# Order, engine and layout changes in a channel attention with two feed-forward networks: two tiles abreast at the start, differences on VectorE, w_in kept in the place of w1, and the last product turned round

## The chip, the cores and the metric

The kernel runs on one core of a Trainium2 chip. The time is device time in microseconds (us) of one execution; a kernel's time is the median of several runs. TensorE (PE) multiplies matrices and loads its weights in separate instructions (PEld), VectorE is DVE, ScalarE is ACT, GpSimd is POOL. SyncE (SP) issues all DMA transfers here. SBUF is the working memory, PSUM holds TensorE's results in eight banks of 128 x 512 float32.

## The reference

There are 6016 tokens of 256 channels. A channel attention gives a 256 x 256 matrix `a`, which multiplies `v`; the first network has 2048 inner columns, the second 1536:

```python
qn = q / (np.linalg.norm(q, axis=1, keepdims=True) + 1e-06)   # k likewise
s = kn.transpose(0, 2, 1) @ qn / tau
a = np.exp(s - s.max(-1, keepdims=True)); a /= a.sum(-1, keepdims=True) + 1e-09
x = v @ a                                    # 6016 x 256
h = x @ w_in                                 # 256 x 2048
g = np.where(h >= 1, h, np.where(h <= -1, 0, (h + 1) ** 2 / 4))
x = g @ w_out                                # 2048 x 256
xn = x / np.sqrt(np.mean(x * x, -1, keepdims=True) + 1e-06) * rms_g
out = (silu(xn @ w_gate) * (xn @ w_val)) @ w_out2   # 256 x 1536, 1536 x 256
```

The five weight matrices arrive as float64.

## The kernel before

**Products in three parts.** Each operand of the networks is kept as a high part in a format of 32 bits that TensorE takes in one pass (fp32r) and a low part, the difference. A product is three matmuls: high by high, high by low, low by high. `split` makes the two parts: a ScalarE copy gives the high one, a subtraction (`sub_hi`, line 86, on VectorE or GpSimd) the low one.

**Attention first.** 14 chunks of q and k are loaded; ScalarE squares them, VectorE sums the squares, TensorE accumulates the scores (line 298). The softmax follows on VectorE and ScalarE. As `v @ a @ w_in` is `v @ (a @ w_in)`, `make_w1` computes w1 = a w_in in four groups of 512 columns, each of two PSUM tiles with six matmuls (line 419).

**Weights.** `fetch` loads 512 KB of float64 (128 x 1024 words) into one of three wide buffers. `narrow` makes float32 of it with four VectorE instructions (lines 158, 162, 166, 174) and two of ScalarE (170, 180), and GpSimd subtracts the high part (line 182). That is one job; there are 34: 8 for w_in, 8 for w_out, 6 each for w_gate, w_val and w_out2. `pump` moves up to two jobs in flight by one stage each and starts one; a job takes five pumps. `require` pumps until given jobs are done. The results for w_in go to two of the eight buffers of a pool (`op`) that also holds the operands of the tiles, so no more than a few groups can wait.

**Tiles and blocks.** Tokens run in 12 tiles, eleven of 512 and one of 384. A tile has 16 blocks ("1", t, f) of the first network and 12 blocks ("2", t, f) of the second. A first block is `emit_A` (six matmuls, line 439), then Relu, Square and a VectorE instruction (lines 449 to 451, `start_g`), then a split (`finish_g`), and three blocks later `emit_B` (six matmuls, line 471). A second block is `emit_GV` (twelve matmuls, line 541), Silu and a product (552, 553), a split, and two blocks later `emit_D`. In `emit_D` the token block is the stationary operand: four blocks of 128 tokens, three matmuls each, 256 columns wide (line 573). `norm` (lines 479 to 524) makes the second network's input from a tile's sums; `prep_v` transposes and splits the next tile's v.

**Order.** A list, `order`, gives the blocks. The 16 first blocks of tile 0 and the first twelve of tile 1 run by themselves; six second blocks of tile 0 (`late`) go among the last four of tile 1. From then on tile t takes the last six second blocks of tile t-2 (`early`) into its first half and the first six of tile t-1 into its second. 18 second blocks are left at the end. After each block, `work` does one stage of a norm or a prep_v and `pump` one stage of the weights. The framework then orders each engine's queue by its own planned times, with the program's order as priority, so instructions can pass others that wait.

**PSUM.** Four banks hold results of A, GV and w1; one pair of banks (`ps_y`) the sums of B, one pair (`ps_o`) those of D.

Of the kernel before, what the change touches and what calls it, by code (L numbers as in the profile page):

```python
# [8 lines left out]
F32 = mybir.dt.float32  # L9
# [7 lines left out]
TOK = 512  # L17
SKEW = 6
LAG = 12
MID = 8  # L20
BLAG = 3
W1_AT = (0, 4, 8)
STAGE = 3
PRE = 2
FLIGHT = 2
# [3 lines left out]

QK_CHUNKS = (2, 2, 4, 4, 4, 4, 4, 4, 4, 4, 4, 3, 2, 2)  # L30

WIDE_MAX = 122879.9921875
# [3 lines left out]
def tile_channel_attention_two_ffn(  # L36
# [35 lines left out]
    ps_mm = ctx.enter_context(tc.tile_pool(name="ps_mm", bufs=4, space=bass.MemoryType.PSUM))  # L72
    ps_y = ctx.enter_context(tc.tile_pool(name="ps_y", bufs=1, space=bass.MemoryType.PSUM))
    ps_o = ctx.enter_context(tc.tile_pool(name="ps_o", bufs=1, space=bass.MemoryType.PSUM))

    def mm_tile(name):
        return ps_mm.tile([P, TOK], F32, tag="mm", name=name)

    def tmp_tile(name):
# [108 lines left out]
    later = []  # L188

# [4 lines left out]
    def narrow_job():  # L194
        if not wide:
            fetch()
        key, x, dst = wide.pop(0)
        if w1_done[0] >= 0:
            while jobs and len(wide) < STAGE - FLIGHT:
# [6 lines left out]
    w1_done = [-1]  # L206

    def may_start():
        key = wide[0][0] if wide else jobs[0][0] if jobs else None
        return key is not None and not (key[0] == "wi" and key[1] > w1_done[0] + 2)  # L210

    def pump():
        for job in flight[:]:
            if next(job, "end") == "end":
                flight.remove(job)
        if len(flight) < FLIGHT and may_start():
            job = narrow_job()
# [8 lines left out]

    wi = {}

    def wi_dst(g, c):
        def dst():  # L230
            if c == 0:
                wi[g] = [opp.tile([P, NC, TOK], F32R, tag="op", name=f"wi{g}_{i}") for i in range(2)]
            return wi[g][0][:, c, :], wi[g][1][:, c, :]
        return dst

# [9 lines left out]

    def wi_jobs(todo, g):
        for c in range(NC):
            todo.append((("wi", g, c), (w_in, c * P, 1), g * TOK, wi_dst(g, c)))

# [6 lines left out]
    NG = F1 // TOK  # L256
    for g in range(2):
        wi_jobs(jobs, g)
    wo_jobs(0)
    for g in range(2, NG):  # L260
        wi_jobs(later, g)
        wo_jobs(g - 1)
    wo_jobs(NG - 1)
    w2 = {}
    for g in range(F2 // TOK):
# [19 lines left out]
    acc = sp.tile([P, 2, JM, C], F32, name="acc")  # L285
    s_ps = [
        ps_y.tile([P, 2, TOK], F32, tag="y", name="s_ps0")[:, 0, :C],
        ps_o.tile([P, 2, 2, C], F32, tag="o", name="s_ps1")[:, 0, 0, :],
    ]
    NQ = len(QK_CHUNKS)  # L290
# [15 lines left out]
    for ci, nj in enumerate(QK_CHUNKS):  # L306
# [28 lines left out]
        if ci >= BEHIND:  # L335
            scores(ci - BEHIND, 1)
    for _ in range(PRE):
        fetch()
    load_v(0)
# [70 lines left out]

    def make_w1(g, b):
        h, l = wi[g]
        ah, al = at[b]
        ps = mm_tile(f"w1_ps{g}_{b}")
        i = 0
        for c in range(NC):
            sl = slice(c * P, (c + 1) * P)
            for x, w in ((ah, h), (ah, l), (al, h)):
                nc.tensor.matmul(ps, x[:, sl], w[:, c, :], start=(i == 0), stop=(i == 3 * NC - 1))
                i += 1  # L420
        sl = slice(g * TOK, (g + 1) * TOK)
        split(w1h[:, b, sl], w1l[:, b, sl], ps)
        if b == NC - 1:
            w1_done[0] = g
            del wi[g]

# [29 lines left out]
    def finish_g(t, f):  # L456
# [3 lines left out]
        gl = spl.tile([P, TOK], F32R, tag="gl", bufs=3, name=f"gl{t}_{f}")  # L460
        split(gh[:, :n], gl[:, :n], r[:, :n], nc.gpsimd if t < 2 or f < 3 else nc.vector)
        g_op[t, f] = (gh, gl)

    def emit_B(t, f):
        _, n = tiles[t]
        if f == 0:
            y_ps[t] = ps_y.tile([P, 2, TOK], F32, tag="y", name=f"y{t}")
        gh, gl = g_op.pop((t, f))
# [95 lines left out]
    def emit_D(t, f):  # L564
        _, n = tiles[t]
        if f == 0:
            o_ps[t] = ps_o.tile([P, 2, 2, C], F32, tag="o", name=f"o{t}")
        uh, ul = u_op.pop((t, f))
        wdh, wdl = w2["dh"], w2["dl"]
        for b in range(n // P):  # L570
            sl = slice(b * P, (b + 1) * P)
            for i, (x, w) in enumerate(((uh, wdh), (uh, wdl), (ul, wdh))):
                nc.tensor.matmul(  # L573
                    o_ps[t][:, b // 2, b % 2, :], x[:, sl], w[:, f, :],
                    start=(f == 0 and i == 0 and b % 2 == 0),
                    stop=(f == NF2 - 1 and i == 2),
                    skip_group_check=True,
                )

    def store(t):  # L580
        n0, n = tiles[t]
        o = o_ps.pop(t)
        nblk = n // P
        for h in range(2):
# [11 lines left out]

    order = []
    m2 = []
    for t in range(NT):
        if t:  # L600
            early, m2 = m2, [("2", t - 1, f) for f in range(NF2)]
            late, m2 = m2[:NF2 - SKEW], m2[NF2 - SKEW:]
        else:
            early, late = [], []
        mid = MID if early else LAG
        for f in range(NF1):
            order.append(("1", t, f))
            if f < mid:
                keep = len(early) * (mid - 1 - f) // mid
                if early:  # L610
                    keep = min(keep, SKEW * (mid - 1 - f) // mid)
                while len(early) > keep:
                    order.append(early.pop(0))
            else:
                keep = (NF2 - SKEW) * (NF1 - 1 - f) // (NF1 - mid)
                while len(late) > keep:
                    order.append(late.pop(0))
    order.append(("flush1",))
    order += m2
    order += [("2", NT - 1, f) for f in range(NF2)]  # L620

    tasks = []

    def work(n_stages=1):
        for _ in range(n_stages):
# [3 lines left out]
            if next(task, "end") == "end":  # L629
                tasks.remove(task)  # L630

    require(*[("wi", 0, c) for c in range(NC)])
    jobs.extend(later)
    for _ in v0:
        pass
    for b in range(NC):
        make_w1(0, b)
    m1, m2 = [], []

    def step1(t, f):  # L640
        if t == 0 and f in W1_AT:
            g = W1_AT.index(f) + 1
            require(*[("wi", g, c) for c in range(NC)])
            for b in range(NC):
                make_w1(g, b)
        ps = emit_A(t, f)
        m1.append((t, f))
        if len(m1) >= 2:
            finish_g(*m1[-2])
        start_g(t, f, ps)  # L650
        if len(m1) > BLAG:
            did_B(*m1[-1 - BLAG])

    def did_B(t, f):
        if t == 0:
            require(("wo", f // 2))
        emit_B(t, f)
        if f == NF1 - 1:
            tasks.insert(0, norm(t))

# [17 lines left out]

    for it in order:
        if it[0] == "1":  # L680
            _, t, f = it
            if f == 0 and t + 1 < NT:
                load_v(t + 1)
            if f == 8 and t + 1 < NT:
                tasks.append(prep_v(t + 1))
            step1(t, f)
            work(1)
            pump()
        elif it[0] == "2":
            while it[1] not in x_op:  # L690
                work(1)
            step2(*it[1:])
            work(1)
            pump()
        else:
            finish_g(*m1[-1])
            for i in range(BLAG, 0, -1):
                did_B(*m1[-i])
            work(2)
    finish_u(*m2[-1])  # L700
# [37 lines left out]
```

## Time and profile before

| | us |
|---|---|
| runs of the kernel | 1218.34, 1219.10, 1219.85 (median 1219.1) |
| the profiled execution: its time | 1220.48 |
| its span, first to last instruction | 1218.7 |
| PE, DVE, ACT, POOL busy in the span | 1179.0, 678.5, 638.3, 179.8 |

Matmuls are pipelined: one of 512 columns is listed with some 390 ns, but the next begins earlier. What one costs is read from the distance between starts, or from the chain of waits, which counts each stretch once. VectorE's entries overlap a little in the same way. A chain piece such as "1.36 PE y L471 x6" says that six matmuls took 1.36 us of the chain.

### The profile page before, as it was taken

What the parts mean: (1) busy time and instruction counts of PE and PEld (TensorE: products, weight loads), DVE (VectorE), ACT (ScalarE), POOL (GpSimd) and SP (SyncE); (2) the same over time, 40 slices, a digit from 0 to 9 for tenths busy, and PEclk for the clock granted to TensorE, in tenths of its full rate; (3) what the DMA queues carried; (4) which work ended last, traced back from release to release, by engine and by line L of the source; (5) the groups of instructions that cost most, each with busy time, mean ns of one, the idle gap of its engine ahead of it and who ended that gap; (6) DMA issues with size and microseconds to landing.
All of it is one profiled execution on the core that took longest, in us unless ns stands there. A gap on an engine that the chain in (4) does not pass through costs nothing.

```text
span 1218.7 us, 15601 instructions
## 1 busy us (share of the span) xinstructions
PE 1179.0 (97%) x6000; PEld 1010.6 (83%) x6000; DVE 678.5 (56%) x977; ACT 638.3 (52%) x1076; POOL 179.8 (15%) x128
## 2 busy tenths in 40 slices
PE   7888789999999999999999999999999999999998
PEld 6666567888888888888888888888888888899998
DVE  5899999464464464364365355355355345445443
ACT  6566776454464455454455455455445445445432
POOL 0255775110010010010010010010010010010000
PEclk9999899999999999999999999999999999999999
DMA  9734433010001001001001001001001000000000
GB/s 352 191 103 121 116 94 85 1 18 18 1 7 29 1 1 35 1 1 35 1 1 36 1 1 35 1 1 35 1 1 31 1 1 18 1 1 18 1 18 14
DMA packets 67275, 43.48 MB, mean 36 GB/s; under 512 B 51456, under 2 KB 57472, under 8 KB 67200
## 3 DMA queue, kind: packets, MB, share of 16 engines
q1 hardware_dynamic: 67200, 42.48, 12.4%
q8 instruction: 47, 0.77, 0.3%
q14 instruction: 28, 0.23, 0.1%
HBM read 36.31 MB, written 6.16 MB: 35 GB/s over the span
## 4 chain that ended last, share of the span: by engine, by line
PE 84%; DVE 7%; DMA 4%; issue 2%; ACT 1%; SPq 1%; POOL 0%; DVEq 0%; POOLq 0%; ACTq 0%
PE y L471 18%; PE h L439 18%; PE o L573 16%; PE vp L541 15%; PE gp L541 15%; DMA qk<-in_q_dram 2%; DVE wide L162 1%; DVE wide L174 1%; DVE wide L158 1%; DVE wide L166 1%; DVE g L451 1%; DMA wide<-in_moe_w_in_dram 1%; SPq L124 1%; DMA wide<-in_moe_w_out_dram 0%; DMA wide<-in_moe_w_val_dram 0%
## 5 line engine op out<-in xcount | busy, mean ns | idle before, releaser
L89 ACT ACTIVATE uh<-u 128x512 fp32r<-128x512 f32 (+1 forms) x144 | 89.8, 624 | 256.1 <-PE o L573 252.4
L86 POOL TENSOR_TENSOR gl<-g,gh 128x512 fp32r<-128x512 f32 (+1 forms) x62 | 85.6, 1384 | 833.0 <-ACT gh L89 619.8
L451 DVE SCALAR_TENSOR_TENSOR g<-h,g 128x512 f32<-128x512 f32 (+1 forms) x192 | 129.6, 676 | 121.6 <-ACT g L450 121.6
L86 DVE TENSOR_TENSOR ul<-u,uh 128x512 fp32r<-128x512 f32 (+1 forms) x144 | 99.2, 689 | 158.5 <-ACT uh L89 158.0
L553 DVE TENSOR_TENSOR u<-u,vp 128x512 f32<-128x512 f32 (+1 forms) x144 | 97.3, 676 | 136.2 <-PE vp L541 133.7
L89 ACT ACTIVATE gh<-g 128x512 fp32r<-128x512 f32 (+1 forms) x192 | 119.0, 620 | 91.6 <-DVE g L451 90.0
L449 ACT ACTIVATE g<-h 128x512 f32<-128x512 f32 (+1 forms) x192 | 112.5, 586 | 93.7 <-PE h L439 92.5
L573 PE MATMUL o<-wdh,ul 128*128 128x256 f32 x564 | 159.6, 283 | 0.0
L573 PE MATMUL o<-wdl,uh 128*128 128x256 f32 x564 | 159.5, 283 | 0.0
L573 PE MATMUL o<-wdh,uh 128*128 128x256 f32 x564 | 158.8, 282 | 0.0
L439 PE MATMUL h<-vh,w1h 128*128 128x512 f32 (+1 forms) x384 | 150.1, 391 | 8.1 <-DVE g L451 7.8
L471 PE MATMUL y<-gh,woh 128*128 128x512 f32 (+1 forms) x384 | 149.7, 390 | 5.4 <-DVE x L485 4.7
L471 PE MATMUL y<-gl,woh 128*128 128x512 f32 (+1 forms) x384 | 149.8, 390 | 1.9 <-POOL gl L86 1.9
L439 PE MATMUL h<-vh,w1l 128*128 128x512 f32 (+1 forms) x384 | 149.3, 389 | 0.0
L471 PE MATMUL y<-gh,wol 128*128 128x512 f32 (+1 forms) x384 | 149.2, 389 | 0.0
L439 PE MATMUL h<-vl,w1h 128*128 128x512 f32 (+1 forms) x384 | 148.3, 386 | 0.0
L86 DVE TENSOR_TENSOR gl<-g,gh 128x512 fp32r<-128x512 f32 (+1 forms) x130 | 91.1, 701 | 76.5 <-ACT gh L89 75.2
L450 ACT ACTIVATE g<-g 128x512 f32<-128x512 f32 (+1 forms) x192 | 119.0, 620 | 4.4
L541 PE MATMUL gp<-xh,wgh 128*128 128x512 f32 (+1 forms) x288 | 111.7, 388 | 3.8 <-DVE g L451 3.6
L541 PE MATMUL vp<-xh,wvh 128*128 128x512 f32 (+1 forms) x288 | 111.2, 386 | 1.6 <-ACT u L552 1.6
L573 PEld LDWEIGHTS o<-wdl,uh 128*128 128x128 f32 x564 | 107.6, 191 | 5.1
L573 PEld LDWEIGHTS o<-wdh,uh 128*128 128x128 f32 x564 | 107.5, 191 | 5.0
(109 smaller groups left out, 2053.3 us busy)
## 6 DMA issues: line engine op xcount, KB each, us to landing
wide<-in_moe_w_out_dram SPq DMA_DIRECT2D x14, 512.0 KB, 3.7
out_dram<-ob SPq DMA_DIRECT2D x23, 256.0 KB, 2.2
vin<-in_v_dram SPq DMA_DIRECT2D x88, 64.0 KB, 2.5
qk<-in_q_dram SPq DMA_DIRECT2D x9, 512.0 KB, 10.2
qk<-in_k_dram SPq DMA_DIRECT2D x9, 512.0 KB, 10.2
wide<-in_moe_w_in_dram SPq DMA_DIRECT2D x8, 512.0 KB, 4.6
wide<-in_moe_w_gate_dram SPq DMA_DIRECT2D x6, 512.0 KB, 3.6
wide<-in_moe_w_val_dram SPq DMA_DIRECT2D x6, 512.0 KB, 3.6
```

What stands on the lines that cost most here:

```text
L86: (eng or nc.vector).tensor_tensor(out=dst_lo, in0=src, in1=hi.bitcast(F32), op=ALU.subtract)
L89: nc.scalar.activation(out=dst_hi, in_=src, func=AF.Copy)
L124: nc.sync.dma_start(out=xv[32 * a:32 * a + 32, c, :n // 32, :], in_=src[a, c])
L158: nc.vector.tensor_scalar(out=high.bitcast(F32), in0=high.bitcast(F32), scalar1=WIDE_MAX, scalar2=-WIDE_MAX, op0=ALU.min, op1=ALU.max,)
L439: nc.tensor.matmul(ps[:, :n], w[:, c, f * P:(f + 1) * P], x[:, c, :n], start=(i == 0), stop=(i == 3 * NC - 1),)
L449: nc.scalar.activation(out=r[:, :n], in_=ps[:, :n], func=AF.Relu, bias=0.5, scale=0.5)
L450: nc.scalar.activation(out=r[:, :n], in_=r[:, :n], func=AF.Square)
L451: nc.vector.scalar_tensor_tensor(out=r[:, :n], in0=ps[:, :n], scalar=1.0, in1=r[:, :n], op0=ALU.max, op1=ALU.min)
L471: nc.tensor.matmul(y_ps[t][:, c, :n], w[:, f, c * P:(c + 1) * P], x[:, :n], start=(f == 0 and i == 0), stop=(f == NF1 - 1 and i == 2),)
L541: nc.tensor.matmul(ps[:, :n], w[:, c, f * P:(f + 1) * P], x[:, c, :n], start=(i == 0), stop=(i == 3 * NC - 1),)
L553: nc.vector.tensor_tensor(out=u[:, :n], in0=u[:, :n], in1=ps[1][:, :n], op=ALU.mult)
L573: nc.tensor.matmul(o_ps[t][:, b // 2, b % 2, :], x[:, sl], w[:, f, :], start=(f == 0 and i == 0 and b % 2 == 0), stop=(f == NF2 - 1 and i ...
```

## The change

The scores' two banks, y and o now come from one pool of two pairs. The jobs for w_in write groups 1 to 3 into `w1h` and `w1l` themselves, where `make_w1` later writes w1; so all eight can be done early, and `PUMPS` lets ten pumps run while q and k are still loaded. The low part of a narrowed weight is taken on VectorE, and that of g on VectorE except for f < 3 of tiles past 3. The blocks of tiles 0 and 1 alternate; the second network begins after four blocks of tile 2 and stays two tiles behind; after the first network's last block 24 second blocks are left. Each block now has one pump, each third block two. D has the weights as the stationary operand (six matmuls 512 wide) except in the last tile, so its result has channels on partitions; `store` transposes it in blocks of 32 x 32 on VectorE and writes it with eight transfers in pieces of 128 bytes, as v is read.

```diff
+PAIR = (1.5, 19.0)
+ALONE = 4
+HELD = 4
-PRE = 2
+PUMPS = (0, 0, 0, 0, 0, 0, 0, 2, 2, 2, 2, 2, 0, 0)
-    ps_y = ctx.enter_context(tc.tile_pool(name="ps_y", bufs=1, space=bass.MemoryType.PSUM))
-    ps_o = ctx.enter_context(tc.tile_pool(name="ps_o", bufs=1, space=bass.MemoryType.PSUM))
+    ps_yo = ctx.enter_context(tc.tile_pool(name="ps_yo", bufs=2, space=bass.MemoryType.PSUM))
...
-        nc.gpsimd.tensor_tensor(out=lo, in0=got, in1=hi.bitcast(F32), op=ALU.subtract)
+        sub_hi(lo, got, hi)
...
+    wi = {0: [opp.tile([P, NC, TOK], F32R, tag="op", name=f"wi{i}") for i in range(2)]}
+    for g in range(1, F1 // TOK):
+        wi[g] = [w[:, :, g * TOK:(g + 1) * TOK] for w in (w1h, w1l)]
...
+    for g in range(NG):
+        wi_jobs(g)
+        wo_jobs(g)
...
         if ci >= BEHIND:
             scores(ci - BEHIND, 1)
-    for _ in range(PRE):
-        fetch()
+        for _ in range(PUMPS[ci]):
+            pump()
...
-        split(gh[:, :n], gl[:, :n], r[:, :n], nc.gpsimd if t < 2 or f < 3 else nc.vector)
+        split(gh[:, :n], gl[:, :n], r[:, :n], nc.gpsimd if t > 3 and f < 3 else nc.vector)
...
+        for c in range(NC):
+            sl = slice(c * P, (c + 1) * P)
+            for i, (w, x) in enumerate(((wdh, uh), (wdl, uh), (wdh, ul))):
                 nc.tensor.matmul(
-                    o_ps[t][:, b // 2, b % 2, :], x[:, sl], w[:, f, :],
+                    o_ps[t][:, c, :n], w[:, f, sl], x[:, :n],
+                    start=(f == 0 and i == 0), stop=(f == NF2 - 1 and i == 2),
                 )
...
+        if t < NT - 1:
+            dst = out[n0:n0 + n, :].rearrange("(b j) (c a i) -> a c j b i", j=32, c=NC, a=4, i=32)
+            for c in range(NC):
+                ob = tmp_tile(f"ob{t}_{c}")
+                nc.vector.transpose(out=ob[:, :n], in_=o[:, c, :n])
+                src = ob.rearrange("p (b i) -> p b i", i=32)
+                for a in range(4):
+                    nc.sync.dma_start(out=dst[a, c], in_=src[32 * a:32 * a + 32, :n // 32, :])
+            return
...
+    at_block = [((f, 0), ("1", 0, f)) for f in range(NF1)]
+    for f in range(NF1):
+        at_block.append(((PAIR[0] + f * (PAIR[1] - PAIR[0]) / (NF1 - 1), 1), ("1", 1, f)))
+    order = [block for _, block in sorted(at_block)]
+    second = [("2", t, f) for t in range(NT) for f in range(NF2)]
+    done = 0
+    for t in range(2, NT):
+        first = ALONE if t == 2 else 0
+        n = NF2 - HELD if t == 2 else NF2 + HELD if t == 3 else NF2
+        base = done
         for f in range(NF1):
             order.append(("1", t, f))
+            while done < base + n * (f + 1 - first) // (NF1 - first):
+                order.append(second[done])
+                done += 1
+    order += [("B",)] * BLAG
+    order += second[done:]
...
+        work(1)
+        pump()
+        if i % 3 == 0:
             pump()
```

## Rows read from the trace of the kernel before

**Rows 1.** The page's 40 slices: VectorE's busy tenths, TensorE's granted clock.
```profile
DVE  5899999464464464364365355355355345445443
PEclk9999899999999999999999999999999999999999
```

**Rows 2.** TensorE's waits from 57.8 to 215 us, first and last of nine.
```profile
PE h L439 <- DVE g L451: 7.8, 7, 1.8
...
PE gp L541 <- ACT u L552: 0.3, 1, 0.3
```

**Rows 3.** The chain that ended last: start us, us, what.
```profile
351.37 2.04 PE h L439 x9
...
547.91 1.43 PE o L573 x12
549.34 1.39 PE h L439 x6
550.73 1.36 PE y L471 x6
...
1010.68 2.04 PE h L439 x9
```

**Rows 4.** TensorE's first w1 matmul and last o matmul, in order of time.
```profile
57.79 2.07 PE L419 MATMUL w_ps<-wi,ah 128*128 128x512 f32 x4
...
1214.40 0.28 PE L573 MATMUL o<-wdh,ul 128*128 128x256 f32 x1
```

**Rows 5.** VectorE's narrowing by line, 57.7 to 205 us: count | busy us, mean ns.
```profile
L166 DVE SCALAR_TENSOR_TENSOR wide<-wide 128x512 uint32<-128x512 uint32 x30 | 30.8, 1028 | 0.2
L174 DVE SCALAR_TENSOR_TENSOR wide<-wide 128x512 uint32<-128x512 uint32 x29 | 28.7, 991 | 0.8 <-ACT wide L170 0.6
L162 DVE TENSOR_SCALAR wide<-wide 128x512 uint32<-128x512 uint32 x30 | 23.6, 786 | 0.0
L158 DVE TENSOR_SCALAR wide<-wide 128x512 f32<-128x512 f32 x30 | 23.2, 774 | 2.8 <-DMA wide<-in_moe_w_in_dram 1.6 <-DMA wide<-in_moe_w_out_dram 0.6 <-DMA wide<-in_moe_w_val_dram 0.5
```

**Rows 6.** VectorE in order of time, 60.68 to 62.57 us, GpSimd idle.
```profile
60.68 0.70 DVE L174 SCALAR_TENSOR_TENSOR wide<-wide 128x512 uint32<-128x512 uint32 x1
61.30 0.68 DVE L166 SCALAR_TENSOR_TENSOR wide<-wide 128x512 uint32<-128x512 uint32 x1
61.90 0.42 DVE L158 TENSOR_SCALAR wide<-wide 128x512 f32<-128x512 f32 x1
62.23 0.42 DVE L162 TENSOR_SCALAR wide<-wide 128x512 uint32<-128x512 uint32 x1
62.57 0.68 DVE L86 TENSOR_TENSOR w1l<-w_ps,w1h 128x512 fp32r<-128x512 f32 x1
```

**Rows 7.** VectorE and GpSimd in order of time around 74 us.
```profile
74.00 1.53 POOL L86 TENSOR_TENSOR gl<-g,gh 128x512 fp32r<-128x512 f32 x1 [0.24 <-ACT gh L89]
74.30 1.78 DVE L174 SCALAR_TENSOR_TENSOR wide<-wide 128x512 uint32<-128x512 uint32 x1
```

**Rows 8.** DMA issues on SyncE's queue, in order of time.
```profile
22.81 0.33 SPq L147 DMA_DIRECT2D wide<-in_moe_w_in_dram  x1
24.14 0.33 SPq L310 DMA_DIRECT2D qk<-in_q_dram  x1
...
28.15 8.82 SPq L124 DMA_DIRECT2D vin<-in_v_dram  x5
37.08 0.42 SPq L310 DMA_DIRECT2D qk<-in_q_dram  x1
```

**Rows 9.** The instructions on the tile vin: duration ns min/median/max.
```profile
L124 SPq DMA_DIRECT2D vin<-in_v_dram x96: 315/487/3522, 28.2 to 931.5; - x96
```

**Rows 10.** One ScalarE line, 57.7 to 205 us.
```profile
L450 ACT ACTIVATE g<-g 128x512 f32<-128x512 f32 x31 | 19.2, 624 | 0.3
```

**Rows 11.** The page's DMA issues: count, KB each, median us to landing.
```profile
out_dram<-ob SPq DMA_DIRECT2D x23, 256.0 KB, 2.2
vin<-in_v_dram SPq DMA_DIRECT2D x88, 64.0 KB, 2.5
```

More of the change, by code (lines that the diff above doesn't have):

```diff
@@ L17 @@
 TOK = 512
-SKEW = 6
-LAG = 12
-MID = 8
+PAIR = (1.5, 19.0)
+ALONE = 4
+HELD = 4
 BLAG = 3
@@ L72, in tile_channel_attention_two_ffn, with yo_tile @@
     ps_mm = ctx.enter_context(tc.tile_pool(name="ps_mm", bufs=4, space=bass.MemoryType.PSUM))
-    ps_y = ctx.enter_context(tc.tile_pool(name="ps_y", bufs=1, space=bass.MemoryType.PSUM))
-    ps_o = ctx.enter_context(tc.tile_pool(name="ps_o", bufs=1, space=bass.MemoryType.PSUM))
+    ps_yo = ctx.enter_context(tc.tile_pool(name="ps_yo", bufs=2, space=bass.MemoryType.PSUM))
     def mm_tile(name):
         return ps_mm.tile([P, TOK], F32, tag="mm", name=name)
+    def yo_tile(name):
+        return ps_yo.tile([P, 2, TOK], F32, tag="yo", name=name)
     def tmp_tile(name):
@@ L186, in tile_channel_attention_two_ffn @@
     ready = set()
-    later = []
     def fetch():
@@ L197, in narrow_job @@
         key, x, dst = wide.pop(0)
-        if w1_done[0] >= 0:
-            while jobs and len(wide) < STAGE - FLIGHT:
-                fetch()
+        while jobs and len(wide) < STAGE - FLIGHT:
+            fetch()
         hi, lo = dst()
@@ L205, in tile_channel_attention_two_ffn @@
     flight = []
[L206 to L210, printed above, removed]
     def pump():
@@ L215, in pump @@
                 flight.remove(job)
-        if len(flight) < FLIGHT and may_start():
+        if len(flight) < FLIGHT and (wide or jobs):
             job = narrow_job()
@@ L224, in require @@
                 pump()
[L227 to L234, printed above, removed]
+    wi = {0: [opp.tile([P, NC, TOK], F32R, tag="op", name=f"wi{i}") for i in range(2)]}
+    for g in range(1, F1 // TOK):
+        wi[g] = [w[:, :, g * TOK:(g + 1) * TOK] for w in (w1h, w1l)]
     def wo_dst(h, l, g):
@@ L244, in gv_dst, with wi_jobs @@
         return lambda: (h()[:, c, g * TOK:(g + 1) * TOK], l()[:, c, g * TOK:(g + 1) * TOK])
-    def wi_jobs(todo, g):
+    def wi_jobs(g):
         for c in range(NC):
-            todo.append((("wi", g, c), (w_in, c * P, 1), g * TOK, wi_dst(g, c)))
+            jobs.append((
+                ("wi", g, c), (w_in, c * P, 1), g * TOK,
+                lambda g=g, c=c: tuple(w[:, c, :] for w in wi[g]),
+            ))
     def wo_jobs(g):
@@ L256, in tile_channel_attention_two_ffn @@
     NG = F1 // TOK
[L257 to L263, printed above, removed]
+    later = []
+    for g in range(NG):
+        wi_jobs(g)
+        wo_jobs(g)
     w2 = {}
@@ L285, in tile_channel_attention_two_ffn @@
     acc = sp.tile([P, 2, JM, C], F32, name="acc")
[L286 to L289, printed above, removed]
+    s_ps = [yo_tile(f"s_ps{b}")[:, 0, :C] for b in range(NC)]
     NQ = len(QK_CHUNKS)
@@ L409, in tile_channel_attention_two_ffn, with make_w1 @@
     woh, wol = w2["oh"], w2["ol"]
[L411 to L420, printed above, removed]
+    def make_w1(g):
+        require(*[("wi", g, c) for c in range(NC)])
+        h, l = wi.pop(g)
+        got = []
+        for b in range(NC):
+            ah, al = at[b]
+            ps = mm_tile(f"w1_ps{g}_{b}")
+            i = 0
+            for c in range(NC):
+                sl = slice(c * P, (c + 1) * P)
+                for x, w in ((ah, h), (ah, l), (al, h)):
+                    nc.tensor.matmul(
+                        ps, x[:, sl], w[:, c, :], start=(i == 0), stop=(i == 3 * NC - 1)
+                    )
+                    i += 1
+            got.append(ps)
         sl = slice(g * TOK, (g + 1) * TOK)
[L422 to L425, printed above, removed]
+        for b in range(NC):
+            split(w1h[:, b, sl], w1l[:, b, sl], got[b])
     y_ps = {}
@@ L466, in emit_B @@
         if f == 0:
-            y_ps[t] = ps_y.tile([P, 2, TOK], F32, tag="y", name=f"y{t}")
+            y_ps[t] = yo_tile(f"y{t}")
         gh, gl = g_op.pop((t, f))
@@ L566, in emit_D @@
         if f == 0:
-            o_ps[t] = ps_o.tile([P, 2, 2, C], F32, tag="o", name=f"o{t}")
+            o_ps[t] = yo_tile(f"o{t}")
         uh, ul = u_op.pop((t, f))
         wdh, wdl = w2["dh"], w2["dl"]
-        for b in range(n // P):
-            sl = slice(b * P, (b + 1) * P)
-            for i, (x, w) in enumerate(((uh, wdh), (uh, wdl), (ul, wdh))):
+        if t == NT - 1:
+            for b in range(n // P):
+                sl = slice(b * P, (b + 1) * P)
+                o = o_ps[t][:, b // 2, (b % 2) * C:(b % 2 + 1) * C]
+                for i, (x, w) in enumerate(((uh, wdh), (uh, wdl), (ul, wdh))):
+                    nc.tensor.matmul(
+                        o, x[:, sl], w[:, f, :],
+                        start=(f == 0 and i == 0 and b % 2 == 0),
+                        stop=(f == NF2 - 1 and i == 2),
+                        skip_group_check=True,
+                    )
+            return
+        for c in range(NC):
+            sl = slice(c * P, (c + 1) * P)
+            for i, (w, x) in enumerate(((wdh, uh), (wdl, uh), (wdh, ul))):
                 nc.tensor.matmul(
-                    o_ps[t][:, b // 2, b % 2, :], x[:, sl], w[:, f, :],
-                    start=(f == 0 and i == 0 and b % 2 == 0),
-                    stop=(f == NF2 - 1 and i == 2),
-                    skip_group_check=True,
+                    o_ps[t][:, c, :n], w[:, f, sl], x[:, :n],
+                    start=(f == 0 and i == 0), stop=(f == NF2 - 1 and i == 2),
                 )
@@ L582, in store @@
         o = o_ps.pop(t)
+        if t < NT - 1:
+            dst = out[n0:n0 + n, :].rearrange("(b j) (c a i) -> a c j b i", j=32, c=NC, a=4, i=32)
+            for c in range(NC):
+                ob = tmp_tile(f"ob{t}_{c}")
[3 more added lines that the diff above has]
+                    nc.sync.dma_start(out=dst[a, c], in_=src[32 * a:32 * a + 32, :n // 32, :])
+            return
+        o = o.rearrange("p a (b c) -> p a b c", c=C)
         nblk = n // P
@@ L594, in store @@
             )
[L597 to L605, printed above, removed]
+    at_block = [((f, 0), ("1", 0, f)) for f in range(NF1)]
[8 more added lines that the diff above has]
+        base = done
         for f in range(NF1):
             order.append(("1", t, f))
[L608 to L620, printed above, removed]
+            while done < base + n * (f + 1 - first) // (NF1 - first):
[3 more added lines that the diff above has]
+    order += second[done:]
     tasks = []
+    n_norms = [0]
     def work(n_stages=1):
@@ L630, in work, with finish_all_g, next_B @@
                 tasks.remove(task)
[L632 to L637, printed above, removed]
+                n_norms[0] = max(0, n_norms[0] - 1)
     m1, m2 = [], []
+    def finish_all_g():
+        for key in list(g_f32):
+            finish_g(*key)
     def step1(t, f):
         if t == 0 and f in W1_AT:
[L642 to L645, printed above, removed]
+            make_w1(W1_AT.index(f) + 1)
         ps = emit_A(t, f)
         m1.append((t, f))
-        if len(m1) >= 2:
-            finish_g(*m1[-2])
+        finish_all_g()
         start_g(t, f, ps)
         if len(m1) > BLAG:
-            did_B(*m1[-1 - BLAG])
-    def did_B(t, f):
+            next_B()
+    def next_B():
+        t, f = m1.pop(0)
+        if (t, f) in g_f32:
+            finish_all_g()
         if t == 0:
@@ L658, in did_B @@
         if f == NF1 - 1:
-            tasks.insert(0, norm(t))
+            n_norms[0] += 1
+            tasks.insert(n_norms[0] - 1, norm(t))
     def step2(t, f):
@@ L677, in did_D @@
             store(t)
-    for it in order:
+    jobs.extend(later)
+    for _ in v0:
+        pass
+    make_w1(0)
+    for i, it in enumerate(order):
         if it[0] == "1":
             _, t, f = it
-            if f == 0 and t + 1 < NT:
+            if t == 0 and f == 1:
+                load_v(1)
+                for _ in prep_v(1):
+                    pass
+            if t > 0 and f == 0 and t + 1 < NT:
                 load_v(t + 1)
-            if f == 8 and t + 1 < NT:
+            if t > 0 and f == 8 and t + 1 < NT:
                 tasks.append(prep_v(t + 1))
             step1(t, f)
-            work(1)
-            pump()
         elif it[0] == "2":
@@ L692, in tile_channel_attention_two_ffn @@
             step2(*it[1:])
-            work(1)
-            pump()
[L695 to L699, printed above, removed]
+        else:
+            next_B()
+        work(1)
+        pump()
+        if i % 3 == 0:
+            pump()
     finish_u(*m2[-1])
```

1 line of the change is left out of this document (removed).

## The prediction

> **What bounds the kernel now.** I read the page's slices first. After slice 8 the clock digit stays at 9 and VectorE is busy about half the time; before that VectorE shows 9 for slices 3 to 7 and the clock dips [rows 1]. So there are two regimes, with a border near 215 us. Next I read who waits for whom on TensorE: from 57.8 to 215 us nine kinds of wait add up to 23.9 us, the first for VectorE's g [rows 2]; after 215 us there is none. The chain of waits then prices TensorE: six matmuls of 512 columns take 1.36 us, 0.2267 each; D's twelve of 256 take 1.43, and the six behind them 1.39 [rows 3]. A D group thus costs 1.46 with its after-effect. The chain's marks at 351.37 and 1010.68 are seven tiles apart, 94.19 us a tile [rows 3].
>
> This can be checked from the code. A tile has 96 matmuls for A, 96 for B, 144 for GV, two for the norm: 338 x 0.2267 = 76.6, and 12 D groups x 1.46 = 17.5; together 94.1. So steady tiles are matmuls and nothing else. All TensorE work from w1 on: 11 x 94.1 = 1035.4; the last tile, with 384 columns at 0.173 (estimated on the line between 0.12 for 256 and 0.2267 for 512), 338 x 0.173 + 108 x 0.12 = 71.4; w1 48 x 0.2267 = 10.9; sum 1117.7. The stretch from the first w1 matmul to the end of the last o matmul is 57.79 to 1214.5 = 1156.7 [rows 4]. So 39.0 us are lost in the first regime: 23.9 in waits, the other 15 in matmuls at less than the full 2.4 GHz, where the clock digit falls to 8 [rows 1]. Behind 1214.5 come 4.2 us of copy and store.
>
> Why VectorE is full there: a job's four VectorE instructions average 1028 + 991 + 786 + 774 = 3.58 us [rows 5]. With GpSimd idle their starts are 0.62, 0.60, 0.33 and 0.34 apart, 1.89 in all [rows 6]. Beside a GpSimd subtraction of 1.53 us the same instruction took 1.78 instead of 0.70 [rows 7].
>
> **The change part by part.**
>
> *D turned round.* Twelve matmuls of 256 become six of 512, of the same shape as y's: 1.46 becomes 1.36, over 11 tiles x 12 = 132 groups 13.2 us. All lie on the path, since steady tiles have no wait. A tile becomes 410 x 0.2267 = 92.9 and TensorE's work 1117.7 - 13.2 = 1104.5. Bounds: 0 and 13.2; I take 13.2, because y in the same rows has this very form. The Trainium skill (TensorE: Matmul & The Clock Gate, section Back-to-back issue gap) gives N/2.4 + 2.5 ns for a matmul of N columns; by that six of 512 are 1.295 us and twelve of 256 are 1.31, and the turn is worth 2 us, not 13. The rows show 0.2267 where it has 0.216, so its constant is too small here.
>
> *Subtractions.* A job costs VectorE 1.89 + 0.60 (a subtraction's distance, as that from 60.68 to 61.30) = 2.5 instead of 3.58, although it now does one instruction more. g's subtraction adds 0.60 per block to 0.60: 1.2. GpSimd keeps only v's first low parts, the norms' small work and f < 3 of late tiles. Behind 215 us the moved subtractions lie in VectorE's idle half; without that cover each would cost 0.6.
>
> *Order.* What counts is VectorE's work against TensorE's up to the last job. Ten pumps during the loads are worth five jobs; 29 stay. The job list has w_in's eight first, so B of the first block (three blocks later) forces nine. After that 4/3 pumps a block, two jobs in four pumps, give 2/3 job a block: the other 25 need 38 blocks, to about the ninth block of tile 2.
> VectorE to there: 29 x 2.5 = 72.5; 41 first blocks x 1.2 = 49.2; three second blocks 3.6; w1's eight subtractions 4.8; two tiles' v, eight instructions, 4.8; one and a third norms of eleven instructions, 8.6. Sum 143.5.
> TensorE: 41 x 2.72 = 111.5; w1 10.9; three second blocks x 4.08 = 12.2; norm 0.5. Sum 135.1.
> VectorE is 8.4 over. In the first four blocks alone it is 19.6 (four jobs 10, four w1 subtractions 2.4, g 4.8, v 2.4) against 10.9, so some 9 are lost at once, and the eager pumps add 4 up to the end of tile 1: 8 to 14 us of waits, I take 11. In the kernel before 23.9 us of waits went with 39.0 of loss; the same ratio gives 18, and I take 20 for queues that are kept in order. Bounds: 8 (the ledger alone) and 39 (nothing gained).
>
> *Start.* By the time q and k are in, some four more weight loads have been issued than before, and the SP queue gives a load 1.33 us [rows 8]: up to 5.3 us later. Against that, the last two chunks wait now behind v's issues, 28.15 to 37.08 [rows 8]; if the fetches take that place and v goes behind, up to 6 us come back. VectorE's three further jobs in this stretch (7 us) find idle time only in part. I take +2, w1 begins at 59.8; bounds -4 and +5.3. Keeping w_in under w1 costs no instruction: w1's two ScalarE copies wait for both PSUM tiles, one of which (1.36) was overlapped before; inside the 20.
>
> *Second network two tiles behind, shared pairs.* y of tiles 0 and 1 hold both pairs; D of tile 0 needs y1's, freed by the first stage of the second norm, some three blocks before. In steady tiles a pair is drained while 12 matmuls of GV and 6 of A stand between, 4.1 us, against two VectorE transposes of some 0.7 (estimated from an instruction of that width [rows 6]). I price this at 0; without the cover it is 1.4 a tile, 15 us. The end runs 24 second blocks by themselves rather than 18, TensorE-bound like the 18.
>
> *Store.* Two issues become eight per tile; v's take 0.487 each [rows 9], so SP is held 3.9 us; only v's and weights' loads stand behind it, not due for half a tile. Priced at 0 for eleven tiles; the last is unchanged.
>
> **Sum.** 59.8 + 1104.5 + 20 + 4.2 = 1188.5 of span. The profiled execution has 1218.7 of span and 1220.48 of time, the median of the runs is 1219.1, 0.4 above that span. I predict 1189.
>
> **Rivals.**
> (a) *ScalarE takes over.* A first block needs three ScalarE instructions at 0.62 [rows 10], a job two, w1, v and norm some 20 in all: 41 x 1.86 + 29 x 1.24 + 3.7 + 12.4 = 128 us against TensorE's 135. With three engines within ten per cent, queued in order, waits add up: the loss stays 39 and the start slips 5.3: 63.1 + 1104.5 + 39 + 4.2 + 0.4 = 1211. For it: VectorE's planned times are missed as soon as one DMA is late; against it: only bursts would be lost.
> (b) *The loss nearly goes.* Weights done early run under the softmax's gaps, the loss is 8 and the start 0: 57.8 + 1104.5 + 8 + 4.6 = 1175. For it: the planner now has no engine that lengthens another's instructions.
> (c) *The turn of D is worth 2 us* (the formula above, in which nearly all of a matmul's time is columns): 1200. For a mechanism here, the cost of 0.10 a group would have to belong to u as a fresh operand and not to the number of matmuls; y with fresh g at 1.36 speaks against it.
> (d) *Slower: the store holds ob.* `ob` takes two of four `tmp` buffers, which g, u and the norm need, for 1.2 (transposes) + 3.9 (issues) + 2.5 (landing as v's [rows 11]) = 7.6 us; the old store landed in 2.2 [rows 11]. If ScalarE stands in its queue for one of them and TensorE follows, eleven stores cost up to 83 us: 1272. It decides (over 1221.5) from 3.0 us a store. Against it: g has three blocks of lag, some 17 us in steady tiles. The Trainium skill (DMA: Bandwidth & Descriptors, Specifications) says that pieces under 512 B are below line rate and are read and written back; if a write so cost twice v's read, the landing would be an estimated 5 us and the hold 10.
>
> **How the numbers follow.** Forecast 57% (1180 to 1199), (a) 17%, (b) 14%, (c) 4%, (d) 6%, and 2% for several small losses that leave it unchanged. The range takes in (c), (a) up to its price, and the slower part of (b): 1174 to 1211. What a measurement can tell from no change is about 0.2%, 2.4 us. Faster: 57 + 17 + 14 + 4 = 92%; within it 2%; slower 6%.
>
> **What the profile after would show.** Right: o in the chain as x6 at 1.36 and marks of one tile 92.9 apart; lines 158 to 174 at 0.42 to 0.70 mean; VectorE still full from 60 to some 190 us, but twelve more first blocks done in it; TensorE's waits down to about 11 us; w1 starting near 60. Wrong: narrowing still at a mean of 0.8 and more (then GpSimd was not the cause); a wait that comes back in every tile (pairs or `ob`); ScalarE full where VectorE was; w1 past 63.

## The result and the profile after

The changed kernel takes 1199.7 us (median of 4 runs, 1198.6 to 1201.7) against 1218.9 us (4 runs) before: ratio 0.9844, 95% interval 0.9827 to 0.9861. The profiled execution took 1198.55 us, its span is 1196.7 us. The prediction was 1189 us, in a range from 1174 to 1211.

The two lines of the page's slices that answer to [rows 1]:

```profile
DVE  5989999746434644644643643653653554544533
PEclk9879998999999999999999999999999999999999
```

VectorE shows 9 in slices 4 to 7 and 8 in slice 3, and the clock still dips, now in slices 2, 3 and 7. TensorE's first w1 and last o matmul, in order of time, answer to [rows 4]:

```profile
68.64 2.07 PE L411 MATMUL w_ps<-wi,ah 128*128 128x512 f32 x4
...
1192.23 0.28 PE L569 MATMUL o<-wdh,ul 128*128 128x256 f32 x1
```

w1 begins 10.9 us later than before, where the prediction had 2. From there to the end of the last o (1192.35, taken as 0.12 after its start, the distance to the matmul before) lie 1123.7 us; less the 1104.5 of matmuls, 19.2 are lost, against a predicted 20. Behind it come 4.35 us.

TensorE's waits from 57 to 215 us (us in all, times, longest), all seven:

```profile
PE a_ps L380 <- DVE s_sb L377: 10.6, 1, 10.6
PE ms L491 <- ACT sh L94: 3.0, 1, 3.0
PE y L464 <- DVE gl L91: 1.8, 1, 1.8
PE h L432 <- DVE g L444: 1.7, 1, 1.7
PE h L432 <- ACT vh L94: 1.6, 1, 1.6
PE y L464 <- ACT gh L94: 0.7, 1, 0.7
PE vp L534 <- ACT u L545: 0.2, 1, 0.2
```

The first stands ahead of w1: TensorE waits for the last step of the softmax. In the kernel before the wait at this place was shorter:

```profile
PE a_ps L391 <- DVE sm L386: 4.1, 1, 4.1
```

The other six lie behind the start of w1, as the nine of [rows 2] do, and add up to 9.0 where those were 23.9. From 215 to 1195 us this view is empty. The steady tiles in the chain (start us, us, what), beside [rows 3]:

```profile
246.34 1.36 PE o L579 x6
...
391.04 2.72 PE h L432 x12
...
948.88 2.72 PE h L432 x12
```

A group of D is six matmuls in 1.36 us, and a tile (948.88 - 391.04) / 6 = 92.97 us. VectorE's narrowing by line, 68 to 205 us (count | busy us, mean ns), beside [rows 5]:

```profile
L179 DVE SCALAR_TENSOR_TENSOR wide<-wide 128x512 uint32<-128x512 uint32 x28 | 19.1, 683 | 0.2 <-ACT wide L175 0.2
L171 DVE SCALAR_TENSOR_TENSOR wide<-wide 128x512 uint32<-128x512 uint32 x27 | 18.4, 680 | 0.0
L163 DVE TENSOR_SCALAR wide<-wide 128x512 f32<-128x512 f32 x26 | 11.0, 422 | 1.8 <-DMA wide<-in_moe_w_out_dram 1.5 <-DMA wide<-in_moe_w_gate_dram 0.3
L167 DVE TENSOR_SCALAR wide<-wide 128x512 uint32<-128x512 uint32 x26 | 10.9, 420 | 0.0
```

The four instructions of a job went from 3.58 to 2.21 us together, by the listed means. What became late is seen in VectorE's queue between the last sums of q and k and w1, in order of time (start us, us, and in brackets idle before and what ended it):

```profile
47.73 0.65 DVE L319 TENSOR_TENSOR acc<-acc 128x512 f32<-128x512 f32 x1
48.30 1.50 DVE L163 TENSOR_SCALAR wide<-wide 128x512 f32<-128x512 f32 x1
49.72 1.50 DVE L167 TENSOR_SCALAR wide<-wide 128x512 uint32<-128x512 uint32 x1
...
60.68 0.73 DVE L371 TENSOR_REDUCE mx<-s_sb 128x1 f32<-128x256 f32 x2
62.60 0.43 DVE L163 TENSOR_SCALAR wide<-wide 128x512 f32<-128x512 f32 x1 [1.18 <-DMA wide<-in_moe_w_in_dram]
...
64.00 0.22 DVE L376 RECIPROCAL sm<-sm 128x1 f32<-128x1 f32 x2
66.33 0.43 DVE L163 TENSOR_SCALAR wide<-wide 128x512 f32<-128x512 f32 x1 [2.12 <-DMA wide<-in_moe_w_in_dram]
66.68 0.42 DVE L167 TENSOR_SCALAR wide<-wide 128x512 uint32<-128x512 uint32 x1
67.01 0.61 DVE L377 TENSOR_SCALAR s_sb<-s_sb,sm 128x256 f32<-128x256 f32 x2
```

The sums end at 48.4 us, in the kernel before at 48.1. But from 48.3 to 60.7 VectorE works at three more weight jobs, among which the steps of the softmax stand (the first two instructions beside a GpSimd subtraction, 1.50 instead of 0.42). Then two narrowings that wait for their load, 1.18 and 2.12 us, stand ahead of the softmax's last product at 67.01, for which TensorE waits 10.6 us. In the kernel before the corresponding steps followed each other from 53.90 to 57.16.

The loads came late because VectorE itself held them up. A load needs one of the three wide buffers, and the buffers became free only with VectorE's subtractions for the jobs before. SyncE's wait for these, and the issue of the two loads:

```profile
SPq L152 <- DVE w1l L91: 7.4, 2, 6.4
...
58.80 1.73 SPq L152 DMA_DIRECT2D wide<-in_moe_w_in_dram  x2
```

### The profile page after: what moved, and what is told of

Its sections match the earlier page's. It is cut to its first block, busy times and chain, and to the rows that moved or that the text cites. A ratio compares the mean times of both kernels' runs of the same rounds, so it can differ in the third digit from the quotient of the medians.

```text
span 1196.7 us, 13950 instructions
## 1 busy us (share of the span) xinstructions
PE 1164.3 (97%) x5208; PEld 971.9 (81%) x5208; DVE 673.5 (56%) x1060; ACT 637.9 (53%) x1065; POOL 71.4 (6%) x56
## 4 chain that ended last, share of the span: by engine, by line
PE 90%; DVE 6%; DMA 3%; ACT 0%; issue 0%; SPq 0%; DVEq 0%; ACTq 0%
PE y L464 20%; PE h L432 20%; PE gp L534 16%; PE vp L534 16%; PE o L579 15%; DMA qk<-in_k_dram 2%; PE o L569 1%; DVE acc L314 1%; DMA wide<-in_moe_w_out_dram 1%; DVE wide L171 1%; DVE wide L167 1%; DMA wide<-in_moe_w_in_dram 1%; DVE wide L179 0%; PE w_ps L411 0%; DVE wide L163 0%
## 5 line engine op out<-in xcount | busy, mean ns | idle before, releaser
L91 DVE TENSOR_TENSOR gl<-g,gh 128x512 fp32r<-128x512 f32 (+1 forms) x168 | 113.4, 677 | 65.6 <-ACT gh L94 63.2
L534 PE MATMUL gp<-xh,wgl 128*128 128x512 f32 (+1 forms) x288 | 110.9, 385 | 0.0
L534 PE MATMUL gp<-xl,wgh 128*128 128x512 f32 (+1 forms) x288 | 110.9, 385 | 0.0
L534 PE MATMUL vp<-xh,wvl 128*128 128x512 f32 (+1 forms) x288 | 110.8, 385 | 0.0
L534 PE MATMUL vp<-xl,wvh 128*128 128x512 f32 (+1 forms) x288 | 110.8, 385 | 0.0
L545 ACT ACTIVATE u<-gp 128x512 f32<-128x512 f32 (+1 forms) x144 | 84.9, 590 | 45.3 <-PE gp L534 26.6
L579 PE MATMUL o<-ul,wdh 128*128 128x512 f32 x264 | 102.9, 390 | 0.0
```

The costliest lines, as they stand in the source:

```text
L91: (eng or nc.vector).tensor_tensor(out=dst_lo, in0=src, in1=hi.bitcast(F32), op=ALU.subtract)
L534: nc.tensor.matmul(ps[:, :n], w[:, c, f * P:(f + 1) * P], x[:, c, :n], start=(i == 0), stop=(i == 3 * NC - 1),)
L545: nc.scalar.activation(out=u[:, :n], in_=ps[0][:, :n], func=AF.Silu)
L579: nc.tensor.matmul(o_ps[t][:, c, :n], w[:, f, sl], x[:, :n], start=(f == 0 and i == 0), stop=(f == NF2 - 1 and i == 2),)
```

## The experiments

All are timed against the kernel before, whose median was 1219.4 to 1220.5 in these comparisons. "w1" is the start of the first w1 matmul; "loss" is the stretch from there to the end of the last o, less the matmuls (1104.5 us with D turned round, 1117.7 without), both of the profiled execution. That one execution took 1.2 us less than the median in the changed kernel and 2.3 more in e10, so small differences of a loss or a sum say little.

| kernel | us | ratio, 95% | w1 | loss | sum |
|---|---|---|---|---|---|
| before | 1219 | 1 | 57.8 | 39.0 | 96.8 |
| changed kernel | 1199.7 | 0.9844 (0.9827-0.9861) | 68.6 | 19.2 | 87.8 |
| e1: before, D turned | 1207.3 | 0.9895 (0.9881-0.9910) | 57.5 | 38.6 | 96.1 |
| e2: before, subtractions on VectorE | 1199.4 | 0.9828 (0.9813-0.9842) | 62.2 | 12.8 | 75.0 |
| e3: changed, D as before | 1210.2 | 0.9917 (0.9902-0.9932) | 68.0 | 18.3 | 86.3 |
| e4: changed, subtractions on GpSimd | 1220.9 | 1.0003 (0.9993-1.0012) | 66.4 | 44.9 | 111.3 |
| e5: before, both of e1 and e2 | 1186.2 | 0.9723 (0.9709-0.9738) | 60.9 | 14.6 | 75.5 |
| e6: changed, weight jobs in old order | 1203.7 | 0.9864 (0.9849-0.9878) | 65.2 | 28.5 | 93.7 |
| e7: changed, no early pumps | 1200.7 | 0.9843 (0.9828-0.9858) | 65.8 | 23.6 | 89.4 |
| e8: changed, one pump a block | 1199.6 | 0.9835 (0.9819-0.9851) | 69.6 | 19.6 | 89.2 |
| e9: changed, old list of blocks | 1196.2 | 0.9801 (0.9781-0.9821) | 68.1 | 17.4 | 85.5 |
| e10: changed, tiles 0 and 1 not alternating | 1202.4 | 0.9859 (0.9841-0.9877) | 68.4 | 25.3 | 93.7 |
| e11: e5, softmax ahead of later jobs | 1192.6 | 0.9774 (0.9758-0.9791) | 57.5 | 24.5 | 82.0 |
| e12: changed, whole old schedule | 1191.4 | 0.9775 (0.9759-0.9792) | 60.8 | 18.7 | 79.5 |

**The parts alone.** e1 gives the kernel before only the new `emit_D` and `store`, e2 only the subtractions:

```diff
-        nc.gpsimd.tensor_tensor(out=lo, in0=got, in1=hi.bitcast(F32), op=ALU.subtract)
+        sub_hi(lo, got, hi)
...
-        split(gh[:, :n], gl[:, :n], r[:, :n], nc.gpsimd if t < 2 or f < 3 else nc.vector)
+        split(gh[:, :n], gl[:, :n], r[:, :n], nc.gpsimd if t > 3 and f < 3 else nc.vector)
```

e5 has both. e3 and e4 take the same parts out of the changed kernel (`if True:` for `if t == NT - 1:` in `emit_D`, and `if False:` in `store`; the two lines above in reverse).

> The kernel before with only D turned round and its transposed store. My theory (each matmul carries a fixed part, a group goes from 1.46 to 1.36 us, 132 groups on TensorE's path): 13 us off, about 1206, tile marks 92.9 to 93.0 apart, no new wait of TensorE after 215 us. Rival (a matmul's time is nearly all columns): 2 us off, 1217. Rival (the store's ob buffers hold up ScalarE): 1222 or more, with a wait in each tile.

> The kernel before with only the subtractions moved to VectorE as in the changed kernel. My theory (a GpSimd subtraction makes VectorE's narrowing wait: 3.58 us a job beside it, 2.5 without it, its own subtraction included): VectorE has about 32 us less for 30 jobs and 18 more for 30 g's, so 10 to 14 us off, about 1207. Rival (the subtractions are load that GpSimd took off VectorE): 60 x 0.6 = 36 us more on the engine that sets the first 200 us, 1250 or so.

> The changed kernel with D and its store as before. My theory: 13 us more than the changed kernel's 1199.7, about 1213, tile marks 94.2 apart, w1 still begins near 68.6. Rival (the turn also costs something, by its store or its transposes, in the first 215 us): less than 10 us more.

> The changed kernel with the subtractions of narrowed weights, and of g as before, back on GpSimd. My theory: 34 jobs x 1.1 = 37 us more of VectorE against about 19 us less for g, so some 18 us more, 1218. Rival (the order alone made the gain of the first stretch and the engine does not matter): within 4 us of 1199.7.

> The kernel before, in its old order and with w_in in its old place, with the subtractions and the turn of D together. Theory A (the two gains are on different stretches and add, and the new order and the early pumps cost): 1199.4 - 13 = about 1186, so 13 us below the changed kernel; w1 begins near 62. Rival (the gains overlap, the order is neutral): 1196 to 1200.

The chain of e1, first and last of eight marks and one group of D:

```profile
347.64 2.04 PE h L439 x9
...
548.58 1.36 PE o L586 x6
...
998.55 2.04 PE h L439 x9
```

(998.55 - 347.64) / 7 = 92.99 a tile, and 13.2 us of time less: the turn is worth what its price said. In e3 it is worth 10.5, between that theory and its rival; of the missing 2.7 us, 1.5 are in the sums of the two profiled executions, and the rest in how these lie to their medians. Narrowing in e4, 68 to 205 us:

```profile
L171 DVE SCALAR_TENSOR_TENSOR wide<-wide 128x512 uint32<-128x512 uint32 x27 | 33.9, 1256 | 0.2
...
L163 DVE TENSOR_SCALAR wide<-wide 128x512 f32<-128x512 f32 x27 | 21.9, 810 | 2.5 <-DMA wide<-in_moe_w_in_dram 1.6 <-DMA wide<-in_moe_w_out_dram 0.8
```

With the subtractions on GpSimd again the same instructions are as long as in [rows 5] or longer, and the time is that of the kernel before. e2 gained 21 us where 10 to 14 had been expected; e4 and e5 came out near their theories.

With D turned, four kernels make a square. Old schedule: 1207.3 (e1) and 1186.2 (e5), so the subtractions are worth 21.1. New schedule: 1220.9 (e4) and 1199.7, 21.2. Read the other way, everything in the change that is neither the turn nor the subtractions (list of blocks, order of the weight jobs, pumps, place of w_in, pairs) costs 13.6 us in both columns. By the ratios, which take out how the kernel before varied between comparisons, the subtractions are worth 21.0 and 19.4 and the rest costs 13.2 and 14.8, so the agreement is closer than the runs can vouch for. e5 beats both kernels, by 33.7 and by 13.6 us.

**Which part of the schedule.** e6 to e10 each undo one part in the changed kernel. e6 puts `w_out`'s jobs back among those of `w_in`; e7 sets all `PUMPS` to 0; e8 drops `if i % 3 == 0: pump()`; e9 builds `order` as before; e10 has this line:

```diff
-    order = [block for _, block in sorted(at_block)]
+    order = [("1", t, f) for t in range(2) for f in range(NF1)]
```

> The changed kernel with the weight jobs in the old order (two groups of w_in, then w_out's and w_in's in turn), everything else kept. Theory B (w_in first makes the first B wait for nine jobs where five would do: four jobs x 2.5 us in front): loss after w1 down by 8 to 10, about 1190. Rival C (the pace of the pumps and the long queue before w1 cost, not which job comes first): within 3 us of 1199.7.

> The changed kernel with no pumps during the loads of q and k. Theory C (three jobs put in VectorE's queue ahead of the softmax make w1 late by 6 us): w1 begins near 62 instead of 68.6, and the total falls by some 4 to 6 us if VectorE's gaps in the softmax take up what was done early. Rival (VectorE is full from 27 us on, so work moved behind the softmax is paid there): w1 earlier, total within 3 us.

> The changed kernel with one pump per block and no second one every third block. Theory C (the pumps run ahead of need, weights of the second network stand in front of g between 160 and 205 us): that stretch's loss of 9 us shrinks, total 4 to 7 lower. Rival B (the loss is the front's nine jobs): within 3 us; or slower, if the second network then waits for its weights.

> The changed kernel with the old list of blocks (tile 0's first network by itself, second network one tile behind), everything else kept: early pumps, w_in under w1, shared pairs, one pump and a second every third block. Theory D (a second block gives TensorE 4.08 us for 1.2 of VectorE, a first block 2.72; as VectorE sets the first 205 us, second blocks and one norm later is what the new list costs): about 1187 to 1190. Rival E (w_in's place, the early pumps or the shared pairs cost it): 1196 or more.

> The changed kernel with tile 1's first blocks all behind tile 0's, the second network still two tiles behind. Theory D (the late second network costs, not the alternation): within 4 us of 1199.7. Rival F (alternating costs, since tile 1's v and both norms come at once in front of or between g's): 1188 to 1194.

Only e9 gains, 3.5 us, where 10 to 13 had been expected. The theories of e6, e7 and e8, that the part named would give back 4 us or more, all failed: e6 is 3.9 us slower, e7 and e8 are within 1 us of the changed kernel. e10 is within the 4 us of its theory. e6 and e7 let w1 begin 3.4 and 2.9 us earlier and pay 9.3 and 4.4 behind it. e7 does not put back the two early fetches of the kernel before: its first load of w_in goes out at 36.78 us, there at 22.81 [rows 8]. So no single part, undone alone, gives back the 13.6.

**Softmax first.** In e5 too VectorE's queue has narrowings ahead of the softmax's last product, and w1 begins 3 us later than before. e11 holds back all jobs past the second, with the rest of the first block, until that product is issued (in the loop over the blocks; in front of it, `require` now finishes only the first two jobs):

```diff
+            if t == 0 and f == 0:
+                load_v(1)
+                with tc.issue_after(soft.ins):
+                    step1(0, 0)
+                    work(1)
+                    pump()
+                continue
```

> The old order with both gains (1186.2), and on VectorE the third and later weight jobs queued behind the last instruction of the softmax. If the wait of a_ps for s_sb (8 us there) is an instruction at the head of VectorE's queue that waits for its w_in load: w1 begins near 57 to 58 instead of 60.9, and 2 to 4 us come off, 1183. Rival (VectorE's sum of work alone counts): w1 earlier, total within 1.5 us of 1186.2.

The first w1 matmul of e11:

```profile
57.45 2.23 PE L419 MATMUL w_ps<-wi,ah 128*128 128x512 f32 x4
```

w1 is 3.5 us earlier, as expected, and the kernel is 6.4 us slower, which neither theory had: 9.9 more are lost later. So the jobs ahead of the softmax in VectorE's queue do delay w1, but holding them back does not pay. Why the later loss grew is not shown. That the held work is due behind w1, where VectorE is full too, is an argument; the granted clock, 0.83 from 160 to 180 us where e5 has 1.00, takes at most 3.4 us there.

**The whole old schedule.** e12 undoes in the changed kernel the list, the job order, the early and the second pumps and the place of the first fetches together. w_in's place with the two tiles' split of w1, tile 1's v (prepared as a whole at tile 0's second block), the shared pairs and the queue of the norms stay.

> The changed kernel with the schedule of before as a whole: the block list of before (one tile at a time, second network close behind the first), the weight jobs in their old order, no early pumps, one pump a block, the first fetches where they were. What stays of the change, beside the subtractions and the turn of D: w_in kept where w1 will lie and the two tiles' weights split together, the inputs of tile 1 prepared at its first block, the shared PSUM pairs. Theory (the schedule costs the 13.5 us as a whole, and its parts hide one another when only one is undone): 1186 to 1189 us, first w1 matmul near 61 us, sum of late start and later loss near 76 us. Rival (the place of w_in, the shared pairs or the inputs of tile 1 cost it): 1194 us or more, first w1 matmul still at 65 us or later.

Neither came true. 1191.4 us lies between: w1 is back at 60.8, as in e5, and 8.3 of the 13.6 us are back. Of these e9 had 3.5 by the list alone; the other 4.8 appear only in this run, in which job order, pumps and fetches go with it. Some 5 us stay with the parts that e12 keeps, as loss behind w1 (18.7 against 14.6 in the profiled executions). Which part it is was not tried, but the trace shows a place: a wait of TensorE at the first product of a norm, as long as in the changed kernel, which e5 does not have.

```profile
PE ms L498 <- ACT sh L94: 3.0, 1, 3.0
```

## Why the prediction was right, and where it was not

1199.7 us lies in the range, but just outside 1180 to 1199, the band to which the prediction gave its 57%; the gain is 19 us where 30 were forecast. That it came so near is in part luck: the rest of the change cost 13.6 us, for which the sum had no such term, and the subtractions gave more than they were priced at.

In spans: 1188.5 predicted, 1196.7 found. w1 came 8.8 later, the loss was 0.8 smaller and the tail 0.15 longer, together 8.2. The rest is that this kernel's median lies 3.0 above that span and not 0.4.

*D turned round*: right. 1.36 a group, 92.97 a tile, 13 us in e1 and in e2 against e5; 10.5 in e3. Rival (c) falls. By the formula that the Trainium skill (TensorE: Matmul & The Clock Gate, Back-to-back issue gap) has for an isolated matmul it would have been worth an estimated 2 us; the runs show 13.

*Subtractions*: that GpSimd lengthens the narrowing was right; the instructions took 0.42 and 0.68 us with GpSimd quiet. The size was too small: alone they are worth 21 us, more than the 19 of loss that the prediction let go by subtractions and order together; the loss of e2 is 12.8. A sum of VectorE's work does not give the 21. The prediction set listed means (3.58) beside distances between starts (1.89; the 0.60 added for a subtraction is 0.62 in the rows it names). Listed against listed a job goes from 3.58 to 2.21 + 0.68 = 2.89 us, so 34 jobs save 23 us, and the 33 subtractions of g up to 205 us take 22 of them back. Over the whole span VectorE is busy 669.6 us in e2 and 678.5 before, 8.9 less. What fell more are TensorE's waits behind w1, from 23.9 to 5.5 us, and the loss to the clock: granted 0.93, 1.00, 1.00, 0.83, 0.91 and 1.00 in the stretches of 20 us from 80 to 200 before, at most 6.6 us, and 1.00 in all of them in e2. How shorter single instructions, at nearly the same sum, make the waits shorter was not tried. TensorE's waits for GpSimd's own g were 1.9 us in all before, so the path of g over GpSimd is not the bulk of it.

*The other 15 us of the kernel before*: the prediction laid them to the clock. With the 6.6 above, 1.4 from 60 to 80 us (0.93) and the half clock of the first two microseconds, the granted clock takes some 9 us at most; the other 6 are neither a listed wait nor the clock.

*Order*: the loss of 20 was met, by errors that cancel. The ledger took five jobs as done for nothing during the loads and charged the eager pumps 4 us. In fact three jobs are done by 39.3 us and three more only among the softmax, and e5 loses 14.6 with the old order and no early jobs, 4.6 less than the new order. VectorE did seven more first blocks by 205 us (38 of g, before 31 [rows 10]), not twelve, and TensorE's listed waits behind w1 are 9.0 us where 11 were taken. The windows of 20 us show when (stretch: us, PE busy (matmuls), PEld, DVE, ACT, POOL, clock, DMA share, GB/s), first the changed kernel, then e5:

```profile
100.00:120.00 20.00, 20.00 (x90) 16.57 (x89) 19.84 (x38) 16.32 (x29) 0.00 (x0) 1.00 0.35 111
...
160.00:180.00 20.00, 16.96 (x74) 13.75 (x73) 18.80 (x35) 15.58 (x29) 0.00 (x0) 0.97 0.34 106
180.00:200.00 20.00, 17.48 (x63) 13.21 (x62) 19.70 (x37) 13.83 (x24) 3.80 (x2) 0.86 0.24 79
```

```profile
100.00:120.00 20.00, 20.00 (x89) 16.08 (x88) 19.24 (x36) 17.32 (x32) 0.00 (x0) 1.00 0.46 124
...
160.00:180.00 20.00, 19.62 (x86) 15.72 (x85) 19.56 (x36) 15.64 (x27) 0.00 (x0) 1.00 0.52 131
180.00:200.00 20.00, 20.00 (x90) 16.57 (x89) 19.24 (x37) 13.51 (x25) 0.00 (x0) 1.00 0.46 133
```

The changed kernel runs from 100 to 160 us without a gap (a full stretch is listed as x90, as matmuls that reach over its borders count in both), and in the next 40 us does 137 of 180: some 9.7 us lost, half of all. Of these 5.5 are waits shown above (ms 3.0, gl 1.8, gh 0.7), and the granted clock of 0.97 and 0.86, where e5 has 1.00, takes 3.4 at most: behind the waits for ms and gl the matmuls start 0.43 us apart for some two microseconds. The clock alone does not set the changed kernel apart, though: e8 has 1.00 in all stretches from 80 to 200 us and loses 19.6. What TensorE waits for hangs in this stretch on VectorE's queue, in the chain one instruction behind the other:

```profile
173.60 0.60 DVE wide L171
174.20 0.60 DVE gl L91
174.80 0.60 DVE sb L483
175.40 0.34 DVE wide L163
175.75 0.33 DVE wide L167
176.08 0.60 DVE wdl L91
```

So the backlog comes late. VectorE is busy 149 us of the stretch from 48 to 205 in the changed kernel and 151 in e5, while TensorE does 559 and 602 matmuls (most of that is the later w1: 7.7 us are 34 matmuls): VectorE's busy time does not tell the two apart. A look at the kinds does not settle it: the changed kernel did 38 of g and none of u there, e5 34 and 8; but e9 did 33 and 6, and only 565 matmuls. What makes the difference stays open.

*Start*: this step failed, in size and outside its bounds (+10.9; bounds -4 and +5.3). The prediction looked at the loads; the q and k sums end within 0.3 us of before. It had written that three further jobs find idle time only in part, and priced 2. They found none behind the sums, and w1 passed the 63 us that the prediction had named as a sign of error: they stand among the softmax (three jobs at an estimated 2.5 us, from the distances in [rows 6] and a subtraction, are 7.5 us, and the two lengthened instructions add 2.2), and two waits for loads (3.3 us) come into its queue. Some of it is not the early pumps: the subtractions alone move w1 by 4.4 (e2), and without early pumps the changed kernel still begins at 65.8 (e7).

*Pairs and store at 0*: no wait after 215 us, as predicted, so rival (d) falls. The page's line for the store:

```profile
out_dram<-ob SPq DMA_DIRECT2D x88, 64.0 KB, 2.0
```

Pieces of 128 bytes landed in 2.0 us, no later than the old store [rows 11], though a transfer now carries a quarter of the bytes. The Trainium skill (DMA: Bandwidth & Descriptors, Specifications) has pieces under 512 B below line rate; no run here tells the rate of such pieces, but whatever they cost, TensorE did not wait for it. Whether the pairs hold up the first tiles is among what e12 left open.

*Rivals (a) and (b)*: ScalarE is busy 116 of the 157 us between 48 and 205, against VectorE's 149, so it did not take over. The loss of 8 us was not reached in any run.

## What to carry to other kernels

Price a change's parts by themselves and again in pairs: here two gave 13 and 21 us, their sum held to half a microsecond, and the rest of the change took 13.6 of it back. Where one engine is full over a stretch, work moved ahead of the stretch's start is free only if that engine really idles there, up to the instruction that opens the stretch; read its queue in order of time across that border, with the loads it would wait for. Start and later loss trade against each other (e6, e7, e11), so judge by their sum.

## What the runs showed of the hardware

After the wait of 10.6 us ahead of w1, the first w1 matmuls start 0.43 us apart and, from 73.06 on, 0.23, 512 columns at 1.2 and at 2.4 GHz; the granted clock from 60 to 80 us, most of the wait included, is 0.67:

```profile
72.22 0.63 PE L411 MATMUL w_ps<-w1h,ah 128*128 128x512 f32 x1
72.64 0.58 PE L411 MATMUL w_ps<-w1l,ah 128*128 128x512 f32 x1
73.06 0.39 PE L411 MATMUL w_ps<-w1h,al 128*128 128x512 f32 x1
73.29 0.39 PE L411 MATMUL w_ps<-w1h,ah 128*128 128x512 f32 x1
```

These 4.4 us at half the clock, ten matmuls, are about 2 us of the 19.2. They are no price of the late start: the kernel before waited 4.1 us at this place and began w1 as slowly, four matmuls in 2.07 us in both [rows 4]. What differs lies later. Behind the wait of 3.0 us for ms the matmuls from 179.85 to 181.98 start 0.43 apart again.

A GpSimd subtraction lengthens VectorE's instructions so much that more instructions there take less time in all: e2 does one instruction more per job and per early g on VectorE, 1049 in all for 977, is busy there 8.9 us less (678.5 to 669.6) and is 21 us faster. The engine's busy time accounts for less than half of that gain.
